# Emitting attention chunks in three stages at set steps of the next recurrence, with gates made further ahead

## The chip, the cores and the metric

The kernel runs on one core of one Trainium2 chip. The metric is the device time of one execution in microseconds (us). TensorE does the matrix products, VectorE, ScalarE and GpSimd the elementwise work, and SyncE issues most of the DMA transfers.

## The reference

Three layers in a row: a gated linear attention (4 batches, 8 heads, 768 tokens, head size 48), a mixture of experts (3,072 tokens, 8 experts, each token to one), and a three-way maxout layer.

```python
mag = np.sqrt(a_re * a_re + a_im * a_im)
scale = np.minimum(mag, 0.999) / (mag + 1e-06)
for t in range(S):                      # 768 tokens
    new_re = ar * S_re - ai * S_im      # ar, ai: a times scale, per head and row
    new_im = ar * S_im + ai * S_re
    kv = np.einsum('bhd,bhe->bhde', k[:, :, t], v[:, :, t])
    S_re, S_im = (new_re + kv, new_im)
    y[:, :, t] = np.einsum('bhd,bhde->bhe', q[:, :, t], S_re)
...
expert_idx = np.argmax(logits, axis=1)
...
out[mask] = gate_w[mask, None] * (np.maximum(x[mask] @ w1[e], 0.0) @ w2[e])
...
h = np.maximum(np.maximum(x @ w1, x @ w2), x @ w3); return h @ w_out
```

## The kernel before

**Recurrence (R0 to R3, one per batch).** `recur` turns the gates of one batch into scaled queries and keys (`QK`). It runs 8 blocks of 8 steps. A step is a multiply (L202) and an add (L215) on VectorE, each needing the one before. Between them `side()` puts one instruction of other work, taken in order from a queue: the norm of the gates for the block ahead (L117, L122, L124, L130, L133, L149, with ScalarE's part at L110 to L150 in between) and the products that write `QK` (L169, L175). Batches after the first hold back the products of their first blocks until the batch before has left the one `QK` buffer. Each block's gates `a` (tile `ain`, 288 KB) and its `qk` rows (`wt`, `pl`, 144 KB each) are loaded from SyncE's queue; `ain` has AB = 4 buffers.

**Chunks (C0 to C3).** When `QK` of a batch is done, `restack` moves it with 18 DMAs on SyncE's queue into two tiles `KQ` (6 x 128 KB, 6 x 256 KB, 6 x 384 KB). Then 6 chunks follow: scores `sc` on TensorE (L361), multiplied by a mask on VectorE into `sT` (L363, two per chunk), the transposed keys `KT`, the state `W` (L385, L392), its scaling `Z` and `t` (L395 on ScalarE, L402 and L408 on VectorE), the output `y` (L427, L430), the token rows `xp` (L504), the choice of the expert (L508 to L516), the rank among the tokens of that expert (L531 to L540), and a scatter of the token rows from GpSimd's queue (L541) into the expert-sorted tensor `xs`. VectorE does this between the steps of the next batch's recurrence. `xs` and parts of `x1o` (printed as `x`) are filled with zeros beforehand by 18 DMAs from GpSimd's queue (L1198, L1204, L1211).

**Expert jobs (P and L).** `moe1` goes over jobs of tokens of one expert, each in 8 pieces `f`: a weight load `wr` of 384 KB (L698, SyncE's queue, WR = 5 buffers), `h` (L730) and `acc` (L754) on TensorE. P is the early jobs (7 jobs, 56 pieces) with batches 0 to 2; L the later ones, with batch 3. The maxout layer follows.

**What sets the order.** `SCHED` lists groups of generators; each group's generators are interleaved by the ratio of their lengths. A scheduler then sorts the instructions of all engines by a simulated timeline, bound by their data and by explicit orders (`issue_order`). Before, P's matmuls and loads are ordered behind the last chunk matmul (`k["pe"]`) and restack DMA (`k["dma"]`) emitted ahead of them.

Of the kernel before, what the change touches and what calls it, by code (L numbers as in the profile page):

```python
# [70 lines left out]
class Attn:  # L71
    def __init__(self, tc, ctx, rctx, consts):
# [5 lines left out]
        self.out = {}  # L78
        self.mark = {}
# [3 lines left out]

        self.gates = [n_p.tile([128, JB, 6 * NC2], F32, name=f"gates{i}") for i in range(2)]
# [7 lines left out]
    def recur(self, b, a_d, qk_d, qe_d):  # L92
# [7 lines left out]
        st = [{} for _ in range(NBLK)]  # L100

        def load(i):
            s, nm = st[i], f"_{b}_{i}"
            s["a"] = self.in_p.tile([128, 2, W], F32, tag="ain", name="ain" + nm, bufs=AB)
            nc.sync.dma_start(s["a"], a_d[b, i].rearrange("p (c w) -> p c w", c=2))
            for c, (w, n) in enumerate((("wt", 2), ("pl", QB))):
                s[w] = self.in_p.tile([128, W], F32, tag=w, name=w + nm, bufs=n)
                nc.sync.dma_start(s[w], qk_d[b, i, :, c * W : (c + 1) * W])
# [3 lines left out]
        def norm(i):  # L112

            s, nm = st[i], f"_{b}_{i}"
            load(i)
            m2, ys = s["sq"][:, 0], s["sq"][:, 1]
            yield tt(out=m2, in0=m2, in1=ys, op=ALU.add)  # L117
            y0 = self.t_p.tile([128, W], F32, tag="y0", name="y0" + nm)
# [23 lines left out]
            third = lambda o: sub(N5, o + 2 * NC2, [[NW, JB], [1, 2], [2, GN]])  # L142
            nc.scalar.copy(out=third(ST), in_=s["wt"].rearrange("p (j d n) -> p j d n", j=JB, d=2))
# [11 lines left out]
        def products(i):  # L155
# [13 lines left out]
            yield own(tt(  # L169
# [27 lines left out]
        def step(i, j):  # L197
# [15 lines left out]
            side()  # L213
# [4 lines left out]
            side()  # L218
# [3 lines left out]
        def line(r, also=None):  # L222
# [6 lines left out]
            last[:] = [r]  # L229

        queue = []

        def side():
            while queue:
                r = next(queue[0], None)
                if r is not None:
                    line(r)
                    return
                queue.pop(0)

        def take(g, n):
            for _ in range(n):
                r = next(g, None)
                if r is not None:
                    yield r

        qe = self.t_p.tile([128, 2, GN], F32, tag="qe", name=f"qe{b}")
        T = at(0)[0]
        nc.gpsimd.memset(T[:, :, 0], 1.0)
        nc.gpsimd.memset(sub(T, 0, [[PJ, GN], [1, 2]]), 0.0)  # L250
        norms = [norm(i) for i in range(NBLK)]
        for r in norms[0]:
            line(r)
        for r in take(norms[1], 1):
            line(r)
        for i in range(NBLK):
            nm = f"_{b}_{i}"
            n1 = norms[i + 1] if i + 1 < NBLK else iter(())
            n2 = norms[i + 2] if i + 2 < NBLK else iter(())

            late = b > 0 and i < 3
            p, *more = [products(x) for x in (((), (), (0, 1))[i] if late else (i - 1,) if i else ())] or [iter(())]
            queue += [take(n1, 2), take(n2, 1), take(p, 1), take(n1, 1), take(p, 1), n1, p, *more]
# [3 lines left out]
            for j in range(JB):  # L267

                while j == JB - 1 and queue:
                    side()  # L270
# [4 lines left out]
            if b == 0 and i >= 2 and self.fill:  # L275
                for _ in range(3):
                    if self.fill:
                        self.fill.pop(0)()
            yield
        self.warm(WARM0.get(b, (0, 0))[0], sub(QK, 0, [[C, 10], [1, 48]]), f"{b}_r")  # L280
# [5 lines left out]
        Tp = at(NBLK)[0]  # L286
        yield

        Te = self.c_p.tile([128, ST], F32, tag="Te", name=f"Te_{b}", bufs=1)
        nc.gpsimd.tensor_copy(out=Te, in_=sub(Tp, 0, [[PJ, 3 * GN], [1, 2]]))  # L290
        nc.gpsimd.tensor_copy(out=k["wend"][:, b * NC2 : (b + 1) * NC2], in_=Te[:, 2 * NC2 :])
        NB1 = NCH - 1
        row = lambda r, d: sub(Te, r, [[d, 2], [2 * NCH, G], [2, NB1]])
        Fr, Fi, Hc, Hx = row(NC2 + 1, 0), row(1, 0), row(NC2 + 2, -NC2), row(2, NC2)
# [23 lines left out]
    def warm(self, n, x, nm):  # L318

        if n:  # L320
            k = self.k
            ps = k["ps_m"].tile([128, 512], F32, tag="am", name="warm" + nm)
            for i in range(n):
                k["pe"] = self.nc.tensor.matmul(ps[:, 0:480], k["ones"], x, start=True, stop=True)  # L324
# [983 lines left out]
```

## Time and profile before

| | |
|---|---|
| runs, device time | 996.64, 996.99, 1002.52 us (median 996.99) |
| profiled execution | 1002.36 us, its span 1000.7 us |
| busy in the span | TensorE 821.3, VectorE 593.2, ScalarE 417.1, GpSimd 144.6 us |
| DMA | 139.20 MB, mean 139 GB/s |
| mean granted clock of TensorE in 184 to 290 us, in 490 to 1000 us | 0.87, 0.99 of full speed |
| chain that ended last, by engine | TensorE 55%, DMA 20%, VectorE 17% |

The span is what the trace covers; 1.7 us of the profiled execution lie around it. The first 389 us are the four recurrences, one behind another; chunks and early expert jobs run beside them. The chunks of the last batch follow up to about 470 us, and from 490 us TensorE works on late expert jobs and the maxout layer. A row of the trace names the engine, the line of the kernel, the output and inputs by their names, shapes as partitions x elements, and the idle time of the engine just before with what ended it.

### The profile page before, as it was taken

Reading aid. Unit: us, or ns where it says so; the run is one execution under the profiler, and the core shown is the slowest. Engines: PE = TensorE matmul, PEld = TensorE weight load, DVE = VectorE, ACT = ScalarE, POOL = GpSimd, SP = SyncE. Lnnn points to the kernel's source line nnn. Section 1 sums busy time; section 2 is a strip of 40 time slices with the busy share of each in tenths; the row PEclk is TensorE's granted clock in tenths of the full one; section 3 lists DMA queues with packets and bytes.
Section 4 is the critical chain, followed back from the end, with each engine's and each line's share of the span. In section 5 each row is a group of like instructions: output and inputs, shape, how many; then the busy total and the mean of one; then the engine's idle time right before and its main releaser. Section 6 shows DMA issues by size and latency. Waiting matters only on the chain.

```text
span 1000.7 us, 15691 instructions
## 1 busy us (share of the span) xinstructions
PE 821.3 (82%) x5490; PEld 723.4 (72%) x5490; DVE 593.2 (59%) x1596; ACT 417.1 (42%) x1045; POOL 144.6 (14%) x230
## 2 busy tenths in 40 slices
PE   1004784769778888789899999998999999999996
PEld 1002674558656776678799999997888888888886
DVE  6989599749984895345667877785232323232222
ACT  5444466336544652335556565563121212121211
POOL 7001011100120012001312222224010101010000
PEclk9999795989788979989899999999999999999999
DMA  9835943995489639942756776662020201020001
GB/s 324 150 104 123 241 130 110 238 242 164 137 269 212 198 94 292 216 131 74 242 177 210 216 215 215 208 210 69 24 64 1 64 1 64 1 64 1 32 1 35
DMA packets 94217, 139.20 MB, mean 139 GB/s; under 512 B 26434, under 2 KB 66770, under 8 KB 94130
## 3 DMA queue, kind: packets, MB, share of 16 engines
q1 hardware_dynamic: 88018, 121.27, 44.0%
q0 software_dynamic: 6112, 16.85, 6.1%
q8 instruction: 45, 0.74, 0.3%
q14 instruction: 42, 0.34, 0.1%
HBM read 93.80 MB, written 22.36 MB: 116 GB/s over the span
## 4 chain that ended last, share of the span: by engine, by line
PE 55%; DMA 20%; DVE 17%; ACT 3%; SPq 2%; issue 2%; POOL 1%; DVEq 0%; ACTq 0%; POOLq 0%
PE h L621 10%; PE h L622 10%; PE h L623 10%; DMA wr<-wm 7%; DMA KQ<-QK 5%; PE acc L621 5%; PE acc L623 5%; PE acc L622 5%; DVE T L202 3%; DMA wt<-qk 2%; DVE T L215 2%; PE h L730 2%; PE acc L754 2%; DMA ain<-a 2%; PE xp L504 1%
## 5 line engine op out<-in xcount | busy, mean ns | idle before, releaser
L865 DVE TENSOR_TENSOR h2s<-h,h2s 128x512 f32<-128x512 f32 x72 | 49.8, 692 | 188.2 <-PE h L623 188.2
L623 PE MATMUL h<-x2h,w2l 128*128 128x512 f32 x324 | 126.6, 391 | 0.0
L622 PE MATMUL h<-x2l,w2h 128*128 128x512 f32 x324 | 126.5, 390 | 0.0
L621 PE MATMUL h<-x2h,w2h 128*128 128x512 f32 x324 | 124.4, 390 | 0.0
L202 DVE TENSOR_TENSOR T<-gates,T 128x216 f32<-128x216 f32 x256 | 97.0, 379 | 4.7 <-ACT gates L147 0.5
L614 ACT CAST h2h<-h2s 128x512 fp32r<-128x512 f32 x36 | 22.3, 620 | 145.4 <-DVE h2s L865 145.4
L730 PEld LDWEIGHTS h<-xh,wr 128*128 128x128 f32 x336 | 51.4, 224 | 36.8 <-DMA wr<-wm 27.3
L621 PE MATMUL acc<-w2h,hh 128*110 128x384 f32 (+2 forms) x200 | 69.3, 348 | 3.9 <-ACT hh L738 3.9
L615 DVE TENSOR_TENSOR w1l<-wr,w1h 128x384 fp32r<-128x384 f32 x72 | 43.7, 607 | 47.7 <-ACT w1h L614 47.5
L623 PEld LDWEIGHTS h<-x2h,w2l 128*128 128x128 f32 x324 | 60.8, 188 | 12.8
L738 ACT ACTIVATE hh<-h 128x128 f32<-128x128 f32 (+5 forms) x128 | 45.8, 359 | 57.3 <-PE h L730 43.6
L622 PEld LDWEIGHTS h<-x2l,w2h 128*128 128x128 f32 x324 | 60.8, 188 | 12.3
L541 POOL DMA_INDIRECT xs<-x,pos x24 | 25.6, 1065 | 304.0 <-DVE T L215 74.0
L730 PE MATMUL h<-xh,wr 128*128 128x128 f32 (+1 forms) x336 | 54.7, 312 | 17.8 <-DMA wr<-wm 16.8
L621 PE MATMUL h<-xh,w1h 128*128 128x330 f32 (+3 forms) x216 | 68.1, 317 | 1.3 <-ACT xh L614 1.2
L621 PEld LDWEIGHTS h<-x2h,w2h 128*128 128x128 f32 x324 | 60.7, 188 | 11.7
L324 PE MATMUL warm_s<-QK,ones 128*128 128x480 f32 x12 | 7.3, 774 | 75.1 <-DVE QK L186 75.1
L622 PE MATMUL acc<-w2l,hh 128*110 128x384 f32 (+2 forms) x200 | 67.9, 341 | 0.0
L622 PE MATMUL h<-xl,w1h 128*128 128x330 f32 (+3 forms) x216 | 67.6, 313 | 0.0
L623 PE MATMUL h<-xh,w1l 128*128 128x330 f32 (+3 forms) x216 | 67.5, 313 | 0.0
L361 PE MATMUL sc<-KQ 96*128 96x128 f32 x384 | 54.5, 294 | 13.8 <-DMA KQ<-QK 12.6
L361 PEld LDWEIGHTS sc<-KQ 96*128 96x128 f32 x384 | 49.3, 203 | 20.3 <-issue 16.6
(204 smaller groups left out, 1967.4 us busy)
## 6 DMA issues: line engine op xcount, KB each, us to landing
wr<-wm SPq DMA_DIRECT2D x128, 384.0 KB
ain<-a SPq DMA_DIRECT2D x32, 288.0 KB
KQ<-QK SPq DMA_DIRECT2D x24, 384.0 KB
w2r<-w SPq DMA_DIRECT2D x24, 384.0 KB
xs<-zero POOLq DMA_DIRECT2D x16, 384.0 KB, 10.2
KQ<-QK SPq DMA_DIRECT2D x24, 256.0 KB
wt<-qk SPq DMA_DIRECT2D x32, 144.0 KB
pl<-qk SPq DMA_DIRECT2D x32, 144.0 KB
```

The lines of the kernel that those rows point to most:

```text
L202: r = tt(out=sub(To, so, [[X, 2], [PJ, 3 * GN], [1, 2]]), in0=sub(N5, j * NW, [[1, NW]]), in1=sub(T, 2 * j, [[0, 2], [PJ, 3 * GN], [1, 2]] ...
L215: r = tt(out=new, in0=new, in1=sub(M, RW + 2 * j, [[-RW, 2], [PJ, GN], [1, 2]]), op=ALU.add)
L361: k["pe"] = nc.tensor.matmul(ps[:, i], Ks[:, h], Qs[:, h], start=True, stop=True)
L541: r = nc.gpsimd.indirect_dma_start(out=self.xs_d, out_offset=bass.IndirectOffsetOnAxis(ap=pos, axis=0), in_=x, in_offset=None, bounds_chec ...
L614: nc.scalar.copy(out=hi, in_=src)
L615: nc.vector.tensor_tensor(out=lo, in0=src, in1=hi, op=ALU.subtract)
L621: r = nc.tensor.matmul(out, ah, bh, start=first, stop=False)
L622: nc.tensor.matmul(out, ah, bl, start=False, stop=False)
L623: nc.tensor.matmul(out, al, bh, start=False, stop=last)
L730: r = nc.tensor.matmul(ps, wh[:, c], xh[:, d, :n], start=d == 0, stop=d == KD - 1)
L738: r = nc.scalar.activation(out=hh[:, :n], in_=ps, func=AF.Relu)
L865: nc.vector.tensor_tensor(out=h, in0=pss[m], in1=h, op=ALU.max)
```

## The change

- **Gates further ahead.** The norm is split in `mag` (three instructions, two blocks ahead, after steps' halves 2, 9 and 11), `scale` (two, at halves 1 and 3) and `gate` (one, at half 4), the latter two one block ahead. They run across the border of a batch: the first two blocks of batch b+1 are prepared in the last blocks of batch b. In batch 0 two loads and the `mag` of block 1 stand ahead of the first step. `ain` goes from 4 buffers to 3, `wt` from 2 to 3, `y0` from 1 to 2.
- **Products.** For batches after the first they begin at the end of block 2, and not within it.
- **Chunks in stages.** A chunk is emitted by `go` from within `recur`, at the steps in `PLACES`: scores; then masks, state sum, token rows, output and ranks; then `t` and `Z`, choice and placing. The first VectorE instruction of masks, `frame` and `choose` is ordered behind the recurrence instruction just emitted (`behind`). The last `PLACES` step is 46 of 64 in each recurrence.
- **Expert jobs.** All P pieces come after R2 or R3 in `SCHED`; their weight loads are ordered behind a named batch's last restack DMA, and their matmuls behind nothing. L's first two pieces were listed ahead of C3; now all stand behind it.
- **Smaller things.** The zero fills go from GpSimd's to SyncE's queue, 3 after each block of R0 from block 1 on, ordered behind that block's load; the last two, 672 and 324 KB from 8 partitions each, stand just ahead of R1's `wt_2` and `ain_2`. Two memsets and the copies of the last state go from GpSimd to VectorE. The warm-up matmuls ahead of C0 (`_s`) are no longer made. Loads of `xt` wait for the scatters of their batch.

```diff
-            for c, (w, n) in enumerate((("wt", 2), ("pl", QB))):
+            for c, (w, n) in enumerate((("wt", 3), ("pl", QB))):
...
+        def mag(b, i):
...
+        def scale(b, i):
...
+        def gate(b, i):
...
+            late = b > 0 and i < 4
+            p = [products(x) for x in (((), (), (0,), (1, 2))[i] if late else (i - 1,) if i else ())]
+            if n2:
+                ld = load(*n2)
+                m = mag(*n2)
+
+            plan.clear()
+            if n1:
+                u = scale(*n1)
+                plan.update({1: u, 3: u, 4: gate(*n1)})
+            if n2:
+                plan.update({2: m, 9: m, 11: m})
+            at_ = [12, 13] if late and i == 2 else [6, 8, 12, 13]
...
+                for g in self.go.get((b, i, j), ()):
+                    next(g)
+            for _ in range(FILL):
+                if b == 0 and i and self.fill:
+                    issue_order(self.tc, self.fill.pop(0)(), ld)
...
+        def behind(r):
+            if self.behind is not None:
+                issue_order(self.tc, r, self.behind)
...
-        for i in range(NCH + 2):
...
+        for i in range(NCH + 3):
             if i < NCH:
                 scores(i)
...
+            yield
+            if i < NCH:
+                masks(i)
             if i < NB1:
-                state(i)
+                add(i)
+            if 0 <= i - 2 < NCH:
+                rows[i - 2] = R.tokens(b, i - 2, yT.pop(i - 2))
             if 0 <= i - 1 < NCH:
                 output(i - 1)
...
+            if 0 <= i - 3:
+                rows[i - 3] = R.ranks(b, i - 3, *rows[i - 3])
             yield
+            if i < NB1:
+                frame(i)
+            if 0 <= i - 2 < NCH:
+                rows[i - 2] = R.choose(b, i - 2, *rows[i - 2], behind)
+            if 0 <= i - 3:
+                self.mark[b, i - 3] = R.place(b, i - 3, *rows.pop(i - 3))
...
-        if GATE > 1 and not k.get("acc"):
-            issue_order(R.tc, r, k["dma"])
+        if not k.get("acc"):
+            issue_order(R.tc, r, k["behind"])
...
-AB = 4
+AB = 3
+FILL = 3
...
-SCHED = [[("R0",)], [("C0",)], [("P", 16)], [("R1",)], [("C1",)], [("P", 20)], [("R2",)], [("C2",), ("R3",)], [("P",)], "L", [("L", 2)], [("C3",)], [("L", 6)]]
+ATS = [9, 14, 19, 25, 31, 37, 40, 43, 45, 46]
+
+PLACES = [divmod(x, JB) for n in range(NCH + 3) for x in (ATS[n], (ATS[n] + ATS[n + 1] + 1) // 2)] + [divmod(ATS[-1], JB)]
+
+SCHED = [[("R0",)], [("C0", 1)], [("R1",)], [("C1", 1)], [("R2",)], ("P", 10, 0), ("P", 14, 1), [("C2", 1)], [("R3",)], ("P", 12, 1), ("P", 20, 2), [("C3",)], "L", [("L", 8)]]
...
-                    lambda h=h: nc.gpsimd.dma_start(
+                    lambda h=h: nc.sync.dma_start(
```

SyncE's queue around the first restack (`KQ_0`, `KQ_3`), at the end of R0. In a name such as `ain_4_1528` the first number is the block and the second a running number; x6 is six instructions in a row. Before:

```order
L108 DMA pl_1_1435<-qk 128x288
L105 DMA ain_3_1489<-a 128x576
L108 DMA wt_2_1452<-qk 128x288
L105 DMA ain_4_1528<-a 128x576
L108 DMA pl_2_1454<-qk 128x288
L108 DMA wt_3_1491<-qk 128x288
L108 DMA pl_3_1493<-qk 128x288
L333 DMA KQ_0_605<-QK_96 16x16x128 x6
L333 DMA KQ_0_605<-QK_96 16x16x256 x6
L333 DMA KQ_3_626<-QK_96 16x16x384 x6
L698 DMA wr_0_0_1237<-wm 128x768
L698 DMA wr_0_1_1245<-wm 128x768
```

After:

```order
L112 DMA wt_2_676<-qk 128x288
L112 DMA pl_1_591<-qk 128x288
L109 DMA ain_2_674<-a 128x576
L112 DMA wt_3_715<-qk 128x288
L109 DMA ain_3_713<-a 128x576
L112 DMA pl_2_678<-qk 128x288
L112 DMA wt_4_838<-qk 128x288
L112 DMA pl_3_717<-qk 128x288
L350 DMA KQ_0_642<-QK_96 16x16x128 x6
L350 DMA KQ_0_642<-QK_96 16x16x256 x6
L350 DMA KQ_3_663<-QK_96 16x16x384 x6
L109 DMA ain_4_836<-a 128x576
```

The gates of block 4 (`ain_4`) stand four places ahead of the restack before, and directly behind its 18 DMAs after.

VectorE in the second block of R1, around the masks of chunk 0 of batch 0 (`sT_0`) before:

```order
L202 TENSOR_TENSOR T<-gates_85,T 128x2x54x2
L363 TENSOR_TENSOR sT_0_0_647<-sc_0_0_642,mask 128x512
L133 TENSOR_TENSOR gates_84<-ain_2_1450,y_1_2_1480 128x16x2x18
L215 TENSOR_TENSOR T<-T 128x36x2
L149 SCALAR_TENSOR_TENSOR sq_2_1456<-sq_2_1456 128x288
L363 TENSOR_TENSOR sT_0_1_654<-sc_0_1_649,mask 128x512
L202 TENSOR_TENSOR T<-gates_85,T 128x2x54x2
L215 TENSOR_TENSOR T<-T 128x36x2
L202 TENSOR_TENSOR T<-gates_85,T 128x2x54x2
L363 TENSOR_TENSOR sT_1_0_706<-sc_1_0_701,mask 128x512
```

VectorE after, from the end of that block into the third, from chunk 0's `t` to chunk 1's first mask; `sq_4` is the first instruction on block 4's gates, after ScalarE's square of `ain_4`:

```order
L433 TENSOR_TENSOR t_0_0_801<-W_0_772,E_655 112x384
L220 TENSOR_TENSOR T<-gates_85,T 128x2x54x2
L439 TENSOR_TENSOR Z_0_789<-Z_0_789,t_0_0_801 112x384
L233 TENSOR_TENSOR T<-T 128x36x2
L220 TENSOR_TENSOR T<-gates_84,T 128x2x54x2
L233 TENSOR_TENSOR T<-T 128x36x2
L140 SCALAR_TENSOR_TENSOR y_1_3_764<-sq_3_719,y_1_3_764 128x288
L220 TENSOR_TENSOR T<-gates_84,T 128x2x54x2
L124 TENSOR_TENSOR sq_4_842<-sq_4_842 128x288
L233 TENSOR_TENSOR T<-T 128x36x2
L141 SCALAR_TENSOR_TENSOR sq_3_719<-sq_3_719 128x288
L403 TENSOR_TENSOR sT_1_0_851<-sc_1_0_811,mask 128x512
```

Chunk 0's masks move from step 11 to step 13 of R1, chunk 1's from step 13 to step 18, and the first instruction on block 4's gates, at step 17, stands ahead of the latter.

TensorE in R2, around the third chunk of batch 1 (`sc_2`); `h` and `acc` are an expert job. After:

```order
L387 MATMUL sc_2_0_1868<-KQ_0_1602 128x128 x4
L778 MATMUL h_0_2_2679<-xh_0_2647,wr_0_2_2677 128x96
L387 MATMUL sc_2_1_1873<-KQ_0_1602 128x128 x4
L778 MATMUL h_0_2_2679<-xh_0_2647,wr_0_2_2677 128x96 x2
L778 MATMUL h_0_3_2688<-xh_0_2647,wr_0_3_2686 128x96 x2
L395 MATMUL kt_2_0_1879<-ident,KQ_0_1602 128x96 x4
L395 MATMUL kt_2_1_1885<-ident,KQ_0_1602 128x96 x4
L778 MATMUL h_0_3_2688<-xh_0_2647,wr_0_3_2686 128x96
L778 MATMUL h_0_4_2697<-xh_0_2647,wr_0_4_2695 128x96 x3
L798 MATMUL acc_0_0_2659<-wr_0_2_2677,hh_0_2_2683 96x384
L778 MATMUL h_0_5_2706<-xh_0_2647,wr_0_5_2704 128x96 x3
```

Before, one expert matmul stands between C1's first scores and its last; after, 14 pieces of P do, and 18 within C2.

## Rows read from the trace of the kernel before

**Rows 1.** Windows: us, busy (count) of PE PEld DVE ACT POOL, PEclk, DMA share, GB/s.

```profile
88.00:184.00 96.00, 72.22 (x615) 59.33 (x615) 82.03 (x273) 51.21 (x142) 12.18 (x19) 0.79 0.66 166
184.00:290.00 106.00, 82.73 (x718) 67.49 (x718) 82.73 (x273) 54.74 (x160) 11.71 (x19) 0.87 0.79 208
290.00:389.00 99.00, 82.24 (x728) 68.06 (x728) 77.06 (x259) 50.69 (x145) 8.30 (x11) 0.91 0.76 194
490.00:1000.00 510.00, 498.88 (x2659) 455.10 (x2657) 235.81 (x433) 180.32 (x392) 77.23 (x68) 0.99 0.31 96
```

**Rows 2.** VectorE by line, 0 to 480 us: busy, mean ns, idle before and its releaser.

```profile
L202 DVE TENSOR_TENSOR T<-gates,T 128x216 f32<-128x216 f32 x256 | 97.0, 379 | 4.7 <-ACT gates L147 0.5
L215 DVE TENSOR_TENSOR T<-T 128x72 f32<-128x72 f32 x256 | 58.7, 229 | 3.8
L363 DVE TENSOR_TENSOR sT<-sc,mask 128x512 f32<-128x512 f32 x48 | 32.8, 687 | 33.4 <-PE sc L361 30.0 <-PE y L427 3.1
L169 DVE TENSOR_TENSOR QK<-pl,T 128x576 f32<-128x576 f32 x32 | 24.0, 751 | 12.7 <-DMA wr<-wm 10.2 <-DMA ain<-a 2.5
L133 DVE TENSOR_TENSOR gates<-ain,y 128x576 f32<-128x576 f32 x32 | 24.0, 750 | 0.0
...
L130 DVE SCALAR_TENSOR_TENSOR y<-sq,y 128x288 f32<-128x288 f32 x32 | 14.5, 452 | 17.6 <-ACT y L126 17.2
...
L402 DVE TENSOR_TENSOR t<-W,E 112x384 f32<-112x384 f32 x20 | 11.0, 551 | 5.9 <-ACT Z L395 5.9
```

**Rows 3.** Timeline of VectorE (start, us): first steps of the recurrences, last product of the fourth.

```profile
12.23 0.39 DVE L202 TENSOR_TENSOR T<-gates,T 128x216 f32<-128x216 f32 x1 [0.49 <-ACT gates L147]
...
86.95 0.37 DVE L202 TENSOR_TENSOR T<-gates,T 128x216 f32<-128x216 f32 x1
...
182.30 0.37 DVE L202 TENSOR_TENSOR T<-gates,T 128x216 f32<-128x216 f32 x1
...
287.69 0.37 DVE L202 TENSOR_TENSOR T<-gates,T 128x216 f32<-128x216 f32 x1
...
388.91 0.27 DVE L186 TENSOR_TENSOR QK<-qe,T 128x72 f32<-128x72 f32 x1
```

**Rows 4.** Waits of VectorE, us, times, longest: in 0:88, in 290:389, in 389:490.

```profile
DVE y L130 <- ACT y L126: 3.5, 1, 3.5
...
DVE sT L363 <- PE sc L361: 8.1, 3, 5.1
...
DVE sT L363 <- PE sc L361: 8.7, 9, 3.4
```

**Rows 5.** Timeline of SyncE's queue: issues of the first and the fourth restack, weights.

```profile
87.91 15.33 SPq L333 DMA_DIRECT2D KQ<-QK  x18
103.28 5.32 SPq L698 DMA_DIRECT2D wr<-wm  x5
...
396.12 0.61 SPq L333 DMA_DIRECT2D KQ<-QK  x1
```

**Rows 6.** Windows over the first restack and over the last zero fills.

```profile
30.00:40.00 10.00, 0.00 (x0) 0.00 (x0) 9.65 (x30) 4.28 (x11) 0.00 (x0) 1.00 1.03 82
40.00:50.00 10.00, 0.00 (x0) 0.00 (x0) 9.37 (x28) 3.07 (x9) 0.00 (x0) 1.00 0.65 93
87.00:112.00 25.00, 19.72 (x136) 15.12 (x137) 18.41 (x57) 10.43 (x28) 3.10 (x6) 0.81 0.97 189
```

**Rows 7.** DMA issues, 0 to 480 us: KB each, median us to landing.

```profile
x<-zero POOLq DMA_DIRECT2D x1, 672.0 KB, 29.4
...
x<-zero POOLq DMA_DIRECT2D x1, 324.0 KB, 28.5
```

**Rows 8.** ScalarE by line, 0 to 480 us: the squares behind each load.

```profile
L110 ACT ACTIVATE sq<-ain 128x576 f32<-128x576 f32 x32 | 21.6, 675 | 3.0 <-DMA ain<-a 2.9
```

**Rows 9.** TensorE by line, 0 to 480 us: the two products of the early expert jobs.

```profile
L730 PE MATMUL h<-xh,wr 128*128 128x128 f32 (+1 forms) x336 | 54.7, 312 | 17.8 <-DMA wr<-wm 16.8 <-ACT xh L682 1.1
...
L754 PE MATMUL acc<-wr,hh 128*128 128x384 f32 (+1 forms) x112 | 49.2, 544 | 2.7 <-ACT hh L738 2.7
```

**Rows 10.** Timeline of TensorE: first batch-3 expert job.

```profile
487.90 0.97 PE L621 MATMUL h<-xh,w1h 128*128 128x360 f32 x2 [1.25 <-ACT xh L614]
```

More of the change, by code (lines that the diff above doesn't have):

```diff
@@ L78, in __init__ @@
         self.out = {}
+        self.stacked = {}
+        self.behind = None
         self.mark = {}
@@ L229, in line, with side @@
             last[:] = [r]
[L231 to L245, printed above, removed]
-        qe = self.t_p.tile([128, 2, GN], F32, tag="qe", name=f"qe{b}")
-        T = at(0)[0]
[L249 to L255, printed above, removed]
+            self.behind = r
+        plan = {}
+        def side(x):
+            if x in plan:
+                line(next(plan[x]))
+        qe = self.t_p.tile([128, 2, GN], F32, tag="qe", name=f"qe{b}")
+        if b == 0:
+            load(0, 0)
+            load(0, 1)
+            for r in (*mag(0, 0), *scale(0, 0), *gate(0, 0), *mag(0, 1)):
+                line(r)
+        T = at(0)[0]
+        line(nc.vector.memset(T[:, :, 0], 1.0))
+        line(nc.vector.memset(sub(T, 0, [[PJ, GN], [1, 2]]), 0.0))
         for i in range(NBLK):
             nm = f"_{b}_{i}"
[L258 to L263, printed above, removed]
+            n1, n2 = ahead(i + 1), ahead(i + 2)
+            late = b > 0 and i < 4
[10 more added lines that the diff above has]
+            at_ = [12, 13] if late and i == 2 else [6, 8, 12, 13]
+            for x in p:
+                plan.update({at_.pop(0): x, at_.pop(0): x})
             after = THR.get(b, {}).get(i)
@@ L323, in warm @@
             for i in range(n):
-                k["pe"] = self.nc.tensor.matmul(ps[:, 0:480], k["ones"], x, start=True, stop=True)
+                self.nc.tensor.matmul(ps[:, 0:480], k["ones"], x, start=True, stop=True)
     def restack(self, b, n, QK):
@@ L374, in scores, with masks, add @@
                 )
-        def state(n):
+        def masks(n):
+            for hf in range(2):
+                s = self.c_p.tile([128, 4, C], F32, tag="sT", name=f"sT{nm(n)}_{hf}", bufs=4)
+                r = nc.vector.tensor_tensor(out=s, in0=S[n][hf], in1=sub(k["mask"], 0, [[0, 4], [1, C]]), op=ALU.mult)
+                if hf == 0:
+                    behind(r)
+                S[n][hf] = s
+        def add(n):
             KT = KTs.pop(n)
-            X = k["ps_m"].tile([112, 4, 2, D], F32, tag="am", name="W" + nm(n))
+            W = X[n] = k["ps_m"].tile([112, 4, 2, D], F32, tag="am", name="W" + nm(n))
             for pr in range(4):
@@ L585, in load @@
             self.tc.declare_no_dep(r.ins, o.ins, reason="distinct rows")
+        for o in self.sc[after]:
+            self.tc.add_manual_dep(
+                r.ins, o.ins.name,
+                mybir.DependencyInfo(mybir.DependencyClass.Sync, mybir.DependencyReason.DATA),
+                reason="the batch's rows",
+            )
         self.ld[after].append(r)
@@ L687, in moe1 @@
     ws = {}
-    def gate(r):
-        if GATE and not k.get("acc"):
-            issue_order(R.tc, r, k["pe"])
     def load(i, f):
```

179 lines of the change are left out of this document (87 added, 92 removed).

## The prediction

> **What bounds the kernel now.** I read the windows by stage first. From 490 us on TensorE is busy 498.9 of 510 us at a granted clock of 0.99: that part has no room, and the change leaves its matmuls as they are. Before it TensorE is busy 72 to 83 us of each hundred or so, so something else sets the pace there [rows 1]. That is VectorE: the timeline shows the recurrences following one another at 86.95, 182.30 and 287.69 us, and the last product of the fourth ends at 388.91 + 0.27 = 389.2 us [rows 3]. What VectorE does between is a chain of steps, and its idle time adds to the chain one for one. So the question is how much earlier the fourth recurrence ends, whether its restack follows at once, and whether the stretch behind that keeps its length.
>
> The lines of VectorE say where it idles [rows 2]: ahead of the masks 33.4 us, nearly all for the scores; ahead of the products L169 12.7, for transfers; ahead of L130 17.6, for ScalarE. Of these, 3.5 us (L130) lie in the first recurrence and 8.7 us (masks) behind the fourth [rows 4]. Three recurrences thus hold 24.7 + 12.7 + 14.1 = 51.5 us of waits in 302.2 us.
>
> **The first recurrence.** Two more instructions of block 1's norm stand ahead of the first step, 0.45 us each by L130's mean [rows 2], with ScalarE's part between them. The cost is 0.9 us at least and about 3 with ScalarE's latency; some small router work that stood between the first steps now lies in that time, and I take 1. The 3.5 us wait goes, since its transfer, a block's `wt`, was late beside the zero fills, which now come block by block. R1 starts at 86.95 + 1 - 3.5 = 84.5.
>
> **The waits removed.** Gates one to two blocks ahead give ScalarE a full block, some 9 us, between the parts of a norm; the waits at L130 should go (14.1). Products begin at the end of block 2, when the restack of the batch before has read `QK`: in R1 the 18 DMAs take 15.33 us to issue [rows 5] and 25 us to move, step 22 comes later than that once the stall below is counted, so the waits at L169 should go (12.7). Masks stand two to five steps later, so most of their 24.7 us goes; but in R2 and R3 pieces of P now stand within the chunks, and I leave 5 us there (both ends: none, and the rival on masks below). Removed: 51.5, left: 5.
>
> **The wait added.** This is the term that decides. With three `ain` buffers, block 4's load stands behind the restack on SyncE's queue, not ahead of it. When does it land? The first restack is issued 87.91 - 86.95 = 1.0 us after its recurrence begins [rows 3, 5]. In the 25 us from 87 to 112 the core moved 189 GB/s, 4.7 MB [rows 6]; the 18 DMAs of the restack are 6 x (128 + 256 + 384) KB = 4.7 MB. So nothing else of size came through in that time. Block 4's 288 KB follow: 1.5 us at that rate, and ScalarE's square 0.68 [rows 8]. VectorE can use it 1.0 + 25 + 1.5 + 0.7 = 28.2 us after the recurrence begins.
>
> When is it wanted? At step 17. By the means of [rows 2]: 17 steps of 0.379 + 0.229 are 10.3; ten instructions of two blocks' norms at 0.45 are 4.5; two gates 1.5; two masks 1.4; `t` and `Z` 1.1: 18.8 us. VectorE takes its instructions in order, so behind `sq_4` all steps, chunk 1's masks and with them TensorE's `y` wait for 28.2 - 18.8 = 9.4 us. The same order stands in R2 and R3, so 3 x 9.4 = 28.2. Ends: nothing, if the load gets in among the restack's packets; about 19 us each in R2 and R3, if five weight loads (5 x 384 KB, 10 us at 189 GB/s) are in the rings ahead. I take 9.4, because the one restack that ran alone is the nearest row. Once this stall has passed, the block's later loads and the second restack tile have it as slack, so I don't add a further wait.
>
> The Trainium skill ("DMA: Bandwidth & Descriptors", Two DMAs through the same engine are not ordered) says that within one queue of one DMA engine descriptors start in order though they may finish out of it. By that rule nothing helps the load past the restack, the stall is there in each of three recurrences, and the time is that of my sum; if rings let later transfers through, it would be 28 us less. The row agrees: 25 us in which only the restack's bytes moved.
>
> **The zero fills.** They cost GpSimd nothing that mattered. The big ones run beside R0's loads. The last two took 29.4 and 28.5 us to land [rows 7]; in 30 to 40 us all DMA engines were busy at 82 GB/s, in 40 to 50 0.65 of them at 93 [rows 6]. Now they stand ahead of R1's `ain_2`, about 20 us before R1 begins, so they are done just in time; I count nothing, and 10 us if one runs behind the other.
>
> The Trainium skill (same page, Why a DMA increments its semaphore by 16 and not by 1) has 8-partition transfers on 8 engines, from SyncE always the lowest-numbered ones, from GpSimd's queue 8 in turn. By that the two fills shared all 16 before and share 8 now, and the sum would be those 10 us higher, 981. The share of 1.03 falling to 0.65 agrees with two sets before; no run yet shows them on SyncE's queue.
>
> **The sum.** The fourth recurrence ends at 84.5 + 302.2 - 51.5 + 28.2 + 5 = 368.4, against 389.2: 20.8 us earlier. Its restack was issued at 396.12 [rows 5], 6.9 us behind, held by P's weight loads ahead of it in the queue. P's last pieces have the same place, but P no longer runs out late by itself; I take a lag of 2 (ends: 0 and 6.9). Gain 25.7. From that restack to the first batch-3 expert job went 487.90 - 396.12 = 91.8 us [rows 5, 10]; the same chunks and nearly the same late pieces lie in it, so I leave it (8 us either way: a longest mask wait of 3.4 twice [rows 4], or as much saved). The rest is TensorE's and moves with it. The profiled execution would go from 1002.36 to 976.7; it lies 0.5% above the median of 996.99, and from the median it is 996.99 - 25.7 = 971.3. I say 971.
>
> **Rivals.**
> *No new stall (a).* If block 4's load comes through with the restack, 28.2 us more are saved: 943. The row on the 25 us speaks against it; that loads and weights were interleaved with later restacks (the windows of R2 and R3 show DMA shares of 0.79 and 0.76, not full) for it.
> *TensorE takes over (b).* Pieces of P cost 54.7/56 + 49.2/56 = 1.86 us busy each [rows 9]. Sixteen ran ahead of C1 before, ten now: 11 us more fall on R2 and R3. TensorE was busy 82.7 + 82.2 = 165 of 205 us there [rows 1], 80%. The two now take some 191 us for 176 of work, 92%. If it can't be filled beyond 80%, because pieces wait for weights in a fixed order (16.8 us of such waits at L730 [rows 9]), they take 220, 29 more: 1000, no change. For it: the order is fixed and the weights stand behind the restack. Against: the granted clock was 0.87 and 0.91 there and 0.99 where TensorE was dense [rows 1], so the work may shrink.
> *Masks wait (c), the other side.* Expert matmuls now stand between the two score halves of a chunk. A matmul waiting for weights holds the scores behind it, the masks wait for the scores, and all steps for the masks. The longest such wait was 5.1 us [rows 4]; at that for each of the 12 chunks in R2 and R3, 61 us instead of 5: 1027. It decides from (1007 - 971 + 5)/12 = 3.4 us per chunk. Against: 24.7 us over 18 chunks were 1.4 each, and the masks are later now.
>
> **How the numbers follow.** About 1% (987 and 1007) is what a measurement of this kernel can tell from no change. My forecast, with its own range of 955 to 987, has 0.5; no stall 0.15; TensorE 0.2, from 988 to 1006, of which a little ends just below; masks 0.13; 0.02 is left. Faster: 0.5 + 0.15 and 0.03 of the TensorE case, 0.68; same 0.19; slower 0.13. The range 945 to 1002 leaves out the masks and the best of the no-stall case.
>
> **What would show it.** In the profile after: a wait of 8 to 11 us at the first `mag` add of block 4, in each of three recurrences, ended by the square of `ain`; no waits at the products, next to none at L140 (L130 before); mask waits of 5 us or less in sum; the fourth recurrence ending near 368; the restack soon after. I am wrong if that stall is absent (then 943), if VectorE waits for scores in R2 and R3 by tens of us, or if R1 starts later than 90 because of the fills.

## The result, and the profile after

The changed kernel took 988.61 us (median of 987.90 to 989.21), the kernel before beside it 997.92: a ratio of 0.9898, interval 0.9865 to 0.9932, 9.3 us or 1.0% faster. The forecast was 971, a gain of 25.7. The direction was right and the size was not: little more than a third of the gain came.

Where each stretch went, by the two traces. The first fence is VectorE's timeline after, the first step of R1, R2 and R3 and the last product of R3, which answer to [rows 3]; the second SyncE's issue of the fourth restack and TensorE's first batch-3 job, which answer to [rows 5, 10].

```profile
87.86 0.39 DVE L220 TENSOR_TENSOR T<-gates,T 128x216 f32<-128x216 f32 x1 [4.33 <-ACT gates L163]
...
183.41 0.38 DVE L220 TENSOR_TENSOR T<-gates,T 128x216 f32<-128x216 f32 x1
...
279.67 0.38 DVE L220 TENSOR_TENSOR T<-gates,T 128x216 f32<-128x216 f32 x1
...
378.03 0.27 DVE L204 TENSOR_TENSOR QK<-qe,T 128x72 f32<-128x72 f32 x1
```

```profile
378.33 0.60 SPq L350 DMA_DIRECT2D KQ<-QK  x1
...
471.52 0.97 PE L674 MATMUL h<-xh,w1h 128*128 128x360 f32 x2 [0.55 <-ACT xh L667]
```

| term | forecast, us | trace after, us |
|---|---|---|
| R1 starts | 84.5 | 87.86 |
| R1, R2 and R3 together, to the last product | 283.9 | 378.30 - 87.86 = 290.4 |
| fourth restack behind that | 2 | 0.0 |
| from it to the first batch-3 job | 91.8 | 471.52 - 378.33 = 93.2 |
| from there to the span's end | 512.8 as before | 986.2 - 471.5 = 514.7 |

The sum of the misses is 3.4 + 6.5 - 2 + 1.4 + 1.9 = 11.2: the trace lost 1000.7 - 986.2 = 14.5 us and not 25.7. The 5.2 us between 14.5 and 9.3 are no term of the kernel: the profiled execution of before, 1002.36, lies 4.4 above the median of 997.92, and that of after, 987.90, lies 0.7 below its own. Which stretch of the first one was long, no trace at the median shows.

The waits are the main thing to see. First the lines of VectorE that answer to [rows 2], to the end of R3 (L403 is the mask, L187 and L140 what L169 and L130 were, L124 and L129 the first two norm instructions); then its longer waits by stage, R1, R2 and R3; then ScalarE's square of block 4's gates in R1, and what ScalarE waited for in R2 ahead of the 5.1 us at L129.

```profile
L187 DVE TENSOR_TENSOR QK<-pl,T 128x576 f32<-128x576 f32 x32 | 24.0, 750 | 0.0
L403 DVE TENSOR_TENSOR sT<-sc,mask 128x512 f32<-128x512 f32 x36 | 23.7, 682 | 1.6 <-PE sc L387 1.4
L140 DVE SCALAR_TENSOR_TENSOR y<-sq,y 128x288 f32<-128x288 f32 x32 | 14.5, 453 | 2.3 <-ACT y L133 2.3
L124 DVE TENSOR_TENSOR sq<-sq 128x288 f32<-128x288 f32 x32 | 14.4, 451 | 30.0 <-ACT sq L114 30.0
...
L129 DVE TENSOR_TENSOR sq<-sq 128x288 f32<-128x288 f32 x32 | 14.4, 451 | 8.5 <-ACT sq L127 8.5
...
L433 DVE TENSOR_TENSOR t<-W,E 112x384 f32<-112x384 f32 x15 | 8.3, 552 | 4.1 <-ACT Z L427 3.8
```

```profile
DVE sq L124 <- ACT sq L114: 9.4, 1, 9.4
...
DVE sq L129 <- ACT sq L127: 5.3, 2, 5.1
DVE sq L124 <- ACT sq L114: 4.3, 1, 4.3
DVE T L220 <- ACT gates L163: 2.1, 1, 2.1
...
DVE sq L124 <- ACT sq L114: 11.9, 1, 11.9
...
DVE sT L403 <- PE sc L387: 0.9, 2, 0.4
```

```profile
116.83 0.68 ACT L114 ACTIVATE sq<-ain 128x576 f32<-128x576 f32 x1 [8.29 <-DMA ain<-a]
...
199.24 0.86 ACT L396 COPY KT<-kt 128x384 f32<-128x384 f32 x2 [4.90 <-PE kt L395]
```

Masks waited 1.6 us in all where they had waited 24.7 in this stretch, products nothing, L140 2.3 after 14.1. All three went as the prediction said. In their place stands the add of block 4's gates: 9.4 us in R1, 4.3 in R2, 11.9 in R3, 25.6 in sum. The forecast was 9.4 in each, 28.2. The 5.1 us at L129 in R2 are not the load's: they come 10.5 us earlier, in block 3's norm, whose square stood on ScalarE behind copies of the transposed keys that waited 4.9 us for TensorE. But time lost there is time that the add behind it need not wait.

By windows, in the columns of [rows 1]: TensorE is busy 77 and 86 us of R2's and R3's 96 and 97, a larger share of each than before.

```profile
88.00:184.00 96.00, 62.28 (x597) 53.64 (x598) 81.11 (x275) 53.25 (x144) 6.96 (x7) 0.84 0.65 167
184.00:280.00 96.00, 76.63 (x700) 64.06 (x699) 80.93 (x273) 55.23 (x157) 10.86 (x13) 0.84 0.84 226
280.00:377.00 97.00, 86.00 (x766) 73.31 (x767) 77.39 (x259) 51.50 (x149) 10.96 (x11) 0.89 0.77 211
```

### The profile page after: what moved, and what is told of

The parts are those of the page before. It is cut to its first block, busy times and chain, and to the rows that moved or that the text cites. A ratio compares the mean times of both kernels' runs of the same rounds, so it can differ in the third digit from the quotient of the medians.

```text
span 986.2 us, 15647 instructions
## 1 busy us (share of the span) xinstructions
PE 807.4 (82%) x5478; PEld 720.1 (73%) x5478; DVE 591.4 (60%) x1608; ACT 423.0 (43%) x1045; POOL 130.4 (13%) x196
## 4 chain that ended last, share of the span: by engine, by line
PE 67%; DVE 14%; DMA 13%; issue 2%; SPq 1%; ACT 1%; DVEq 0%; ACTq 0%
PE h L674 10%; PE h L676 10%; PE h L675 10%; DMA ain<-a 6%; PE acc L674 6%; PE acc L675 5%; PE acc L676 5%; PE sc L387 4%; DVE T L220 3%; PE h L778 3%; PE acc L798 3%; DMA KQ<-QK 2%; DVE T L233 2%; PE xp L536 2%; PE y L458 2%; DMA xt<-xs 2%
## 5 line engine op out<-in xcount | busy, mean ns | idle before, releaser
L387 PE MATMUL sc<-KQ 96*128 96x128 f32 x384 | 63.8, 327 | 109.0 <-DMA KQ<-QK 89.2
L387 PEld LDWEIGHTS sc<-KQ 96*128 96x128 f32 x384 | 58.0, 234 | 113.6 <-issue 93.1
L587 POOL DMA_INDIRECT xs<-x,pos x24 | 29.2, 1216 | 308.0 <-DVE sq L132 63.1
L233 DVE TENSOR_TENSOR T<-T 128x72 f32<-128x72 f32 x256 | 58.8, 230 | 4.3
L778 PE MATMUL h<-xh,wr 128*128 128x128 f32 (+1 forms) x336 | 51.5, 299 | 7.3 <-DMA wr<-wm 6.2
```

Source lines behind the costliest of these rows:

```text
L233: r = tt(out=new, in0=new, in1=sub(M, RW + 2 * j, [[-RW, 2], [PJ, GN], [1, 2]]), op=ALU.add)
L387: nc.tensor.matmul(ps[:, i], Ks[:, h], Qs[:, h], start=True, stop=True)
L587: r = nc.gpsimd.indirect_dma_start(out=self.xs_d, out_offset=bass.IndirectOffsetOnAxis(ap=pos, axis=0), in_=x, in_offset=None, bounds_chec ...
L778: nc.tensor.matmul(ps, wh[:, c], xh[:, d, :n], start=d == 0, stop=d == KD - 1)
```

## The experiments

Each ratio is to runs of the kernel before on the same chip. R1's and R2's lengths are from first step to first step, R3's to its last multiply, each in one trace. Two traces of one kernel differ by up to 3.6 us in a recurrence, so a smaller difference shows nothing by itself.

| run | ratio (interval) | R1 starts | R1 | R2 | R3 | first batch-3 job |
|---|---|---|---|---|---|---|
| before | 1 | 86.95 | 95.4 | 105.4 | 98.7 | 487.90 |
| before, again | 0.9993 (0.9974 to 1.0012) | 87.02 | 99.0 | 105.7 | 100.7 | 492.94 |
| changed | 0.9898 (0.9865 to 0.9932) | 87.86 | 95.6 | 96.3 | 95.0 | 471.52 |
| changed, again | 0.9903 (0.9886 to 0.9921) | 87.80 | 96.4 | 99.0 | 93.6 | 474.59 |
| four ain buffers | 0.9796 (0.9760 to 0.9833) | 83.59 | 97.6 | 95.7 | 94.5 | 464.91 |
| wide fills | 0.9841 (0.9805 to 0.9877) | 83.79 | 96.0 | 97.8 | 93.5 | 468.58 |
| block 4 from GpSimd | 0.9782 (0.9747 to 0.9816) | 87.87 | 93.6 | 95.6 | 93.7 | 467.56 |
| four buffers, wide fills | 0.9789 (0.9761 to 0.9816) | 82.94 | 94.0 | 94.6 | 94.8 | 458.38 |
| the same, chunks later | 0.9876 (0.9848 to 0.9903) | 83.49 | 93.5 | 95.2 | 93.1 | 474.14 |
| no explicit order (`behind`) | 0.9920 (0.9888 to 0.9952) | 87.71 | 100.3 | 92.0 | 93.4 | 472.12 |
| block 4 from GpSimd, wide fills | 0.9765 (0.9732 to 0.9798) | 83.46 | 93.1 | 96.4 | 92.9 | 463.10 |
| blocks 4 and 5 from GpSimd, wide fills | 0.9729 (0.9698 to 0.9760) | 83.33 | 95.7 | 92.5 | 94.8 | 463.14 |
| fills on GpSimd | 0.9908 (0.9871 to 0.9944) | 89.76 | 96.3 | 98.3 | 95.0 | 476.65 |

### Block 4's load ahead of the restack

```diff
-            for c, (w, n) in enumerate((("wt", 3), ("pl", QB))):
+            for c, (w, n) in enumerate((("wt", 2), ("pl", QB))):
...
-            y0 = s["y0"] = self.t_p.tile([128, W], F32, tag="y0", name=f"y0_{b}_{i}", bufs=2)
+            y0 = s["y0"] = self.t_p.tile([128, W], F32, tag="y0", name=f"y0_{b}_{i}", bufs=1)
...
-AB = 3
+AB = 4
```

> The changed kernel with four ain buffers again (and, to make room, two wt and one y0 buffer), so that block 4's load stands ahead of the restack on SyncE's queue. Theory A (the load behind the restack is what costs): the waits at the first mag add of block 4, 9.4 + 4.3 + 11.9 us in R1 to R3 of the changed kernel, fall below 2 us each, and the time drops by 18 to 28 us from 988.6, to 961 to 971. Rival B (the stall only hides what comes next: block 5's load and wt of block 4 now stand behind the restack): a wait of 5 us or more appears at block 5's add or at the gate of block 4 in each recurrence, and the time drops by less than 10 us. Rival C (the transfers are short of bandwidth, not of order): the restack ends later by what the load takes, the masks wait instead, time within 3 us of 988.6.

The ratio went from 0.9898 to 0.9796, some 10 us. But look at what did it. The waits of VectorE in R1 of this run:

```profile
DVE sq L129 <- ACT sq L127: 8.5, 5, 5.8
DVE t L433 <- ACT Z L427: 4.4, 1, 4.4
```

The wait at block 4's add is gone, as theory A had it, and R1 is not shorter (97.6 us): 8.5 us now stand at L129, 4.4 at `t`. R2 and R3 didn't shorten either. What moved is the start: R1 begins at 83.59, since in the new order of SyncE's queue the load of `ain_2` stands ahead of the last zero fills. So rival B was nearer than A, with the wait in another place than it said. ScalarE's timeline of that run shows whose wait it is:

```profile
97.98 0.48 ACT L396 COPY KT<-kt 128x384 f32<-128x384 f32 x1 [6.14 <-PE kt L395]
...
101.58 0.46 ACT L127 ACTIVATE sq<-y 128x288 f32<-128x288 f32 x1
...
114.80 0.68 ACT L114 ACTIVATE sq<-ain 128x576 f32<-128x576 f32 x1 [5.22 <-DMA ain<-a]
```

ScalarE takes its instructions in order. L396 copies transposed keys of the first chunk and waits 6.1 us for TensorE, whose scores wait for the restack's data; the square L127, which L129 needs, stands behind it. Then block 5's square (L114) waits 5.2 us for its load, which now is the one behind the restack, and the first `Z` of the next chunk stands behind that.

### The zero fills

```diff
-                    x1_d.rearrange("(e s) d -> e s d", e=NE)[:, CAP:], pview(z, 0, 0, [1, NE], [[0, RS - CAP], [1, DM]])
+                    x1_d.rearrange("(e s) d -> s e d", e=NE)[CAP:], pview(z, 0, 0, [1, RS - CAP], [[0, NE], [1, DM]])
...
-                    x1_d[e * RS + lo : e * RS + CAP].rearrange("(p a) d -> p a d", p=8),
-                    pview(z, 0, 0, [1, 8], [[0, (CAP - lo) // 8], [1, DM]]),
+                    x1_d[e * RS + lo : e * RS + CAP].rearrange("(p a) d -> p a d", p=72),
+                    pview(z, 0, 0, [1, 72], [[0, (CAP - lo) // 72], [1, DM]]),
```

> The changed kernel with the last two zero fills spread over 56 and 72 partitions instead of 8 each; all else the same. Theory A (the two fills of 8 partitions hold SyncE's queue for 20 us ahead of R1's loads): the issues of R1's wt, pl and ain behind them take 0.4 us each and not 4.4, the 4.3 us wait at R1's first step is gone, R1 starts near 84 instead of 87.9 us, and the time drops by 3 to 5 us, to 984 to 986. Rival B (any fill of that size ahead of the loads holds them): the wait stays over 3 us and the time is within 1.5 us of 988.6.

SyncE's issues behind the two fills, in the changed kernel and then with wide fills (start, duration):

```profile
61.60 0.56 SPq L1250 DMA_DIRECT2D x<-zero  x1
62.61 0.81 SPq L1257 DMA_DIRECT2D x<-zero  x1
64.80 3.11 SPq L112 DMA_DIRECT2D wt<-qk  x1
68.02 4.38 SPq L112 DMA_DIRECT2D pl<-qk  x1
72.49 4.44 SPq L109 DMA_DIRECT2D ain<-a  x1
77.02 4.43 SPq L112 DMA_DIRECT2D wt<-qk  x1
81.55 2.11 SPq L109 DMA_DIRECT2D ain<-a  x1
```

```profile
61.94 0.65 SPq L1250 DMA_DIRECT2D x<-zero  x1
63.03 0.94 SPq L1257 DMA_DIRECT2D x<-zero  x1
65.14 1.81 SPq L112 DMA_DIRECT2D wt<-qk  x1
67.89 0.85 SPq L112 DMA_DIRECT2D pl<-qk  x1
68.85 0.36 SPq L109 DMA_DIRECT2D ain<-a  x1
73.68 0.33 SPq L112 DMA_DIRECT2D wt<-qk  x1
```

After two issues of 1.8 and 0.9 us a DMA's issue takes 0.33 to 0.36 us in the second; in the first four take 3.1 to 4.4 and a fifth 2.1: the queue itself is held behind the fills, and R1's first loads are issued until 83.7. R1 starts at 83.79 and not 87.86, and the ratio falls by 0.0057. Theory A held, rival B fell.

> The changed kernel with the zero fills back on GpSimd's queue, as before; all else as changed. By the prediction's step the wait of 3.5 us in R0 comes back (a block's wt late beside the fills) and R1 starts near 86 to 88; if SyncE's queue with the 8-partition fills cost 4.4 us at R1's first step, that wait is gone. Both about cancel: time within 3 us of the changed kernel.

This undoes one part: all fills go back to GpSimd's queue (`nc.sync.dma_start` becomes `nc.gpsimd.dma_start` in the three places). R0's wait comes back, larger, at the first multiply of a block (5.3 and 1.4 us); the 4.3 us at R1's first step are gone; R1 starts at 89.76, later than the 86 to 88 expected, and the time is the changed kernel's. So the move to SyncE bought about nothing as it was made.

### The same load from another queue

```diff
-            nc.sync.dma_start(s["a"], a_d[b, i].rearrange("p (c w) -> p c w", c=2))
+            q = nc.gpsimd if b and i == 4 else nc.sync
+            q.dma_start(s["a"], a_d[b, i].rearrange("p (c w) -> p c w", c=2))
```

> The changed kernel, with block 4's gates in R1 to R3 loaded from GpSimd's queue instead of SyncE's; still three ain buffers, so the load can't start before the recurrence has begun, and moves while the restack does. Theory A (place in SyncE's queue and rings): the load lands well inside the restack, the waits at block 4's add fall from 9.4, 4.3 and 11.9 to under 3 us each, time 965 to 978. Rival C (DMA engines are full with the restack, whoever issues): the load lands with the restack's end, the waits stay over 6 us in R1, time within 4 us of 988.6.

GpSimd's issue and ScalarE's square on the load, and the waits of R1:

```profile
91.72 0.58 POOL L110 DMA_DIRECT2D ain<-a  x1 [4.72 <-ACT sq L115]
...
104.72 0.71 ACT L115 ACTIVATE sq<-ain 128x576 f32<-128x576 f32 x1
```

```profile
DVE t L434 <- ACT Z L428: 5.4, 2, 3.4
DVE y L141 <- ACT y L134: 3.0, 2, 2.3
```

Issued at 91.7, in the middle of the restack, the load was there by 104.7, when ScalarE got to it; in the changed kernel its square began at 116.8. So it is the place behind the restack in SyncE's queue that made it late, not DMA engines too full to take it: theory A, and rival C fell. The Trainium skill ("DMA: Bandwidth & Descriptors", Queues, rings and completion order) says that an engine with work in several rings takes them in turn; these rows agree. The ratio is 0.9782. Yet with 9.4, 4.3 and 11.9 us taken away no recurrence got shorter by more than 3.4, against either trace of the changed kernel; in R1 `t` now waits 5.4.

### Both repairs, and the better versions

> Both: four ain buffers (two wt, one y0) and the wide fills. If the two causes are apart, the gains of the two single runs add: 957 to 968 by theory A for both. If they share a wait (a later start of R1 gives block 4's load more time), the sum is short by the shared part, and the time is that of the better single run.

0.9789, the same as four buffers alone: they share the wait at R1's first step, so the gains don't add. Against wide fills alone (0.9841) the removal of some 26 us of stall was worth about 5.

> The changed kernel with both cheap repairs: block 4's gates of R1 to R3 loaded from GpSimd's queue, and the last two zero fills spread over 56 and 72 partitions. Theory G (the recurrence is held by the landing of the restack and of what stands behind it, so a wait taken away comes back in part as another): 4 to 7 us off the kernel with the GpSimd load alone, ratio 0.970 to 0.975 to the kernel before; R1 to R3 together 282 to 285 us long, R1 starting at 83 to 84. Rival (gains as far apart as their waits): below 0.965.

0.9765 and R1 to R3 of 282.3 us, with R1 starting at 83.46: theory G, a little short in its gain (3.1 us by medians against the GpSimd load alone, not 4 to 7).

> As the one before, and block 5's gates too from GpSimd's queue. Theory H (what holds the recurrence next is block 5's load behind the restack): another 5 us or more off, ratio below 0.969. Theory G (it is the restack's data, which chunk work on ScalarE and VectorE needs before the norm's later parts run): within 3 us of the run with block 4's load alone.

0.9729: the fastest version here, 1.7% under the changed kernel (condition `i in (4, 5)` in the diff above). The intervals of the two overlap, and R1 to R3 are the same 283 us, so theory H isn't shown.

### What holds the recurrence then

> Four ain buffers and wide fills, with half of each restack left out: only the first of the two parts (c = 0) is moved, the other rows of KQ hold a constant set by GpSimd, so later layers work on other numbers and only the recurrences are to be compared. Theory G (recurrences are held by the restack's landing): the restack's 9 DMAs move in some 13 us, the waits of R1 (3.8 at L129, 3.9 at t, some 10 in all) fall below 4, R1 is 85 to 89 us long instead of 94; R2 and R3, where TensorE's expert pieces also wait for weights, shorten by 3 to 8 each. Rival (the waits are ScalarE's and TensorE's own time): R1 stays over 92.

```diff
         t = self.s_p.tile([96, H, 2, RC * C], F32, tag="KQ", name=f"KQ_{b}_{n}")
+        self.nc.gpsimd.memset(t, 0.05)
         for lo, hi in SPLITS[n > 0]:
-            for c in range(2):
+            for c in range(1):
```

R1 fell from 94.0 to 88.0 us, and its waits, in the first fence, from 11.5 to 5.0 us; in the second those of the same kernel with the whole restack. (The whole time, 13676.85 us in the one run, tells nothing, since the later layers work on other numbers.)

```profile
DVE sq L129 <- ACT sq L127: 2.7, 3, 2.1
DVE y L140 <- ACT y L133: 2.3, 1, 2.3
```

```profile
DVE sq L129 <- ACT sq L127: 5.3, 4, 3.7
DVE t L433 <- ACT Z L427: 3.9, 1, 3.9
DVE y L140 <- ACT y L133: 2.3, 1, 2.3
```

R1 is thus held by the restack's arrival, whichever instruction takes the wait. The loads behind the restack came earlier too; but block 5's alone, taken out of the queue above, had not shortened R1 (95.7 against 93.1).

R2 and R3 were no shorter (96.0, 95.8), but the run can't tell what the restack costs there, for its constants have a price of their own. Each recurrence has two memsets on GpSimd of 5.2 us; here is one from R2 and one from R3, with the row of VectorE's choice of the expert (`OH`) beside it:

```profile
252.72 5.21 POOL L347 MEMSET KQ<- 96x6144 f32 x1 [2.15 <-issue]
254.51 3.46 DVE L559 TENSOR_SCALAR OH<-em,e 128x8 bf16<-128x8 f32 x1
...
354.88 5.24 POOL L347 MEMSET KQ<- 96x6144 f32 x1
355.90 4.25 DVE L559 TENSOR_SCALAR OH<-em,e 128x8 bf16<-128x8 f32 x1
```

`OH`, whose median is 0.23 us, ended within 0.1 us of the memset's end each time (2.36 and 3.46 us in R2, 3.73 and 4.25 in R3), and the steps behind it with it (in R1 one took 1.27); with the whole restack none takes more than 0.30. That is 5.4 and 7.5 us of stretched instructions. Without them R2 and R3 would be about 90.6 and 88.3 us by subtraction, 4 and 6.5 shorter than with the whole restack and within theory G's 3 to 8; it is an estimate, as waits here don't simply add, and no run shows it. VectorE's waits fell there too, from 11.5 to 9.1 and from 16.9 to 11.0 us.

> Four ain buffers and wide fills, and all 56 early expert pieces ordered behind the third restack, so that R2 runs with chunks and restack alone, as R1 does, and the pieces come in R3 and behind it. Theory G (the restack's landing holds a recurrence): R2 stays at 91 to 95 us, within 3 of the 94.6 with pieces in it. Theory B (TensorE and the weights of the pieces hold R2): R2 falls to 86 to 90, R3 grows. In both the pieces then lack cover, and the first batch-3 job comes 15 us or more later than at 458.4; the time is over 985.

```diff
-SCHED = [[("R0",)], [("C0", 1)], [("R1",)], [("C1", 1)], [("R2",)], ("P", 10, 0), ("P", 14, 1), [("C2", 1)], [("R3",)], ("P", 12, 1), ("P", 20, 2), [("C3",)], "L", [("L", 8)]]
+SCHED = [[("R0",)], [("C0", 1)], [("R1",)], [("C1", 1)], [("R2",)], [("C2", 1)], [("R3",)], ("P", 56, 2), [("C3",)], "L", [("L", 8)]]
```

R2 took 91.8 us against 94.6 with pieces in it, within what theory G allowed: with the restack whole, the pieces add at most some 3 us, no more than two traces of the changed kernel differ in R2 (96.3 and 99.0). That R2 would fall further with neither was not tried. What the pieces do cost appears behind R3, which ended at 360.1, six us earlier. Matmuls of the pieces from then on, first here, then with the pieces where the change has them:

```profile
L778 PE MATMUL h<-xh,wr 128*128 128x128 f32 (+1 forms) x222 | 33.4, 291 | 9.3 <-DMA wr<-wm 9.1
```

```profile
L778 PE MATMUL h<-xh,wr 128*128 128x128 f32 x40 | 5.9, 282 | 2.4 <-DMA wr<-wm 2.3
```

222 against 40 matmuls, 37 pieces against 7, and the first batch-3 job at 505.63 instead of 458.38; the time was 1018.9 in one run, beside 1003.67 for the kernel before.

### Where the chunks stand

```diff
-ATS = [9, 14, 19, 25, 31, 37, 40, 43, 45, 46]
+ATS = [15, 20, 25, 30, 36, 41, 44, 47, 49, 50]
```

> Four ain buffers and the wide fills, and the stages of the chunks begun six steps later in each recurrence (first at step 15 and not 9, last at 50 and not 46). Theory D (with the load early the recurrence waits for the restack all the same, through the chunk's work: ScalarE's copies of the transposed keys wait for scores of data in transfer, and the norm's squares stand behind them): the waits at L129 (5.8, 4.1, 7.7 us) and at t (4 us) fall to half, each recurrence is 4 to 8 us shorter, R3 ends 12 to 20 us earlier than with the steps of the change, time 960 to 970. Rival E (what is late is the loads of blocks 5 and on behind the restack): the same waits stay at the same steps, time within 3 us of 979. Rival F (the later end of the chunks delays expert jobs and TensorE takes over): recurrences shorten but the first batch-3 job doesn't come earlier.

On top of four buffers and wide fills. The three recurrences shortened by 1.5 us in sum, not by 12 to 20, so theory D fell; the first batch-3 job came 15.8 us later, at 474.14, and the ratio rose to 0.9876. That is what rival F forecast: more of the expert pieces lie behind R3 (71 matmuls of `h`, against 40). That chunks which end later release their tokens later is its reason, and fits, but wasn't tested by itself. (Some 5 of the 15.8 are the execution: the trace with 458.38 is of 974.12 us, that kernel's median 979.49.)

> The changed kernel without the explicit order of chunk work behind the recurrence's steps (behind does nothing; the stages and their places in the program stay). Theory: the scheduler puts masks earlier again and they wait for scores, some 10 to 20 us more of mask waits in R1 to R3, time 992 to 1002. Rival: the places of emission alone hold the order, the waits are the same and the time is within 3 us of the changed kernel.

```profile
DVE sT L402 <- PE sc L386: 7.3, 3, 3.4
DVE sq L124 <- ACT sq L114: 3.5, 1, 3.5
```

Without the explicit order (`behind` does nothing) masks wait again, 7.3 us in R1, as the theory said, and the add of block 4 only 3.5 where it had waited 9.4. But the time is what the rival said: 0.9920 lies within the interval of the changed kernel. The explicit order moves a wait from the masks to the add; in a kernel that has the stall it brings nothing that shows.

### The kernels again

> The kernel before once more, unchanged, for a second trace: the profiled execution that the prediction was worked from was 5 us above its median. Theory: the second trace lies near 997 to 1000 and its recurrences end 2 to 5 us earlier than 389.2, with the same waits (restack's QK, masks, L130) in the same places, so the forecast's terms were read off a slightly long execution. Rival: it is the stretch behind 490 us that varies; then the recurrences end within 1 us of 389.2. Ratio to the kernel before 1.000 within its interval.

The second trace of before is longer still, span 1006.5, with the same waits. Its batch-3 job starts at 492.94, 513.6 us before its end, as far as in the first (512.8); so what differs between these two lies in the recurrences: they end 5.9 us later, and R1 took 99.0 us for 95.4. The theory that the second trace would be shorter fell; its point, that a stretch read off one execution of this kernel is uncertain by some 5 us, stands.

> The changed kernel once more, unchanged, beside the other runs of this call: ratio to the kernel before 0.988 to 0.992, as at first; the waits at block 4's add again 9, 4 to 9 (with the wait just ahead of it at the mult of block 3) and 12 us in R1 to R3.

The ratio came again, 0.9903, with 7.9, 5.7 and 11.4 us at block 4's add.

## Why the prediction was right and wrong

**Right: the waits that go, and the one that comes.** The steps on masks, products and L130 held (51.5 us to some 4), and so did the mechanism of the stall: block 4's load lands behind the restack, 25.6 us in sum for 28.2. That R1's 9.4 us came out to a tenth is luck. The load could be used 29.7 us after the recurrence began (forecast 28.2), mainly since the restack began 2.1 us and not 1.0 after it, and VectorE wanted it at 20.3 (forecast 18.8), after 2.3 us of small waits that the sum of its work did not have: two errors of 1.5 us that cancel. The order is the one that the Trainium skill's rule gives ("DMA: Bandwidth & Descriptors", Two DMAs through the same engine are not ordered), and these rows agree with it.

**Wrong: "I don't add a further wait", and "left 5".** The prediction took the rest of the recurrence to have the stall as slack. In the trace after, other waits of 17.6 us stood in R1 to R3: at L129 (5.3), at `t` (3.8), at L140 (2.3), at the first step of a block (2.1), at the masks (1.5) and at smaller places (2.6). With the 25.6 they are 43.2 us of waits for 33.2 forecast; the rest of the three recurrences was 247.2 us long where the forecast had 250.7, so that 6.5 of the 10.0 remain. The step took waits as separate sums. They are not: in R1 the restack's arrival stands behind most of them, and half a restack shortened R1 by 6. Rival (a), "943 without the stall", failed for the same reason, and it is the larger error, though it was not the forecast: with the stall taken away in two ways the time fell by 5 to 12 us and not 28. R1 to R3 shortened by some 5 in sum, from 286.8 to 289.5 in four traces with the stall (changed, again, wide fills, fills on GpSimd) to 282.3 to 283.3 in four without it, and not at all with four buffers alone (287.8).

**Wrong: the zero fills ("I count nothing").** They cost 4.3 us at R1's first step. R1 started 3.4 us late against the forecast, and making them wide was worth 0.0057 of the time and brought R1 to 83.79. (The first step of R0 came 2.5 us later than before, at 14.71, where 1 was forecast; R0 from there on was 2.4 us shorter, its waits aside, and made that up.) The case was in the text as a bound of 10 us, with the reason: 8-partition transfers from SyncE share 8 engines (the Trainium skill, "DMA: Bandwidth & Descriptors", Why a DMA increments its semaphore by 16 and not by 1). In the trace after, the 22 us from 62 on show a DMA share of 0.55 at 88 GB/s, where on GpSimd's queue the share was 1.03 and then 0.65 [rows 6]; this agrees with it. I chose "just in time" against that. What neither said is that the issue of the next DMAs on the queue takes 3 to 4 us meanwhile.

**Wrong: the base.** A gain read off an execution of 1002.36 was taken from a median of 996.99. By the traces 14.5 us went; between medians 9.3. That is 5.2 us of the miss, the second largest term.

**Small terms.** No lag of the fourth restack (2 forecast), 1.4 us more to the first batch-3 job, 1.9 more behind it. Together with 3.4, 6.5 and 5.2 this makes 16.4, the whole of 25.7 - 9.3.

**The other rivals.** TensorE did not take over in the change: R2 and R3 took 194.9 us to the last product, 191 had been worked out, and 220 if it had. Its work there was 164.2 us and not 176: between the first steps of R2 and the last multiply of R3 the trace before has 244 matmuls of `h` and the trace after 254, under two pieces more and not six (six matmuls to a piece). It is near, though: the later chunks and the later pieces both lost more behind R3 than the recurrences had gained. The rival on masks fell: 1.5 us in R2 and R3, where 3.4 per chunk would have been needed.

What stays open: how much of R2 and R3, 92 to 99 us when restack, expert pieces and norm all meet, is the restack's and how much the pieces'. The half restack was disturbed there by its own memsets, and pieces taken out of R2 shortened it by 3 us, within what two traces differ.

## What to carry to other kernels

Waits in one chain that all end with the same transfer, as most in R1 do here, are one wait: price what is left when the first of them goes (when does the data come, and what is the next instruction that needs it), not each by its own row. When a buffer is given away, look in the queue's order for the transfer that now stands behind a long one; another queue for that one transfer can be the cheapest repair. Don't subtract from a median a stretch that was read off an execution which is itself off the median. And when an experiment leaves work out, see in its trace what the stand-in costs: here a memset on GpSimd hid what it was to show in two recurrences of three.

## What the runs showed of the hardware

Two transfers from 8 partitions, 996 KB together, held SyncE's queue itself: the four DMAs behind them took 3.1 to 4.4 us each to issue and the fifth 2.1, and with the same bytes from 56 and 72 partitions 1.8, 0.9 and then 0.33 to 0.36. A load issued from GpSimd's queue 1.8 us after the restack had begun, whose 18 DMAs need 25 us [rows 6], was used 13 us later, while on SyncE's queue it came behind all of them. A VectorE instruction of 0.23 us (`OH`, a tensor_scalar that writes bf16) that started within a GpSimd memset of 5.2 us took 2.36 to 4.25 us in R2 and R3, to the memset's end.
